# Two weight loads issued by SyncE, a list scheduler that counts SyncE's transfers by their rows, and new order constants, in a fused attention and Mish feed-forward kernel

## The chip, the cores and the metric

The kernel runs on one core of one Trainium2 chip. The metric is the device time of one execution in microseconds (us); the time before is the median of three runs, 942.09 us (940.99 to 942.83). TensorE is called PE, VectorE DVE, ScalarE ACT, GpSimd POOL and SyncE SP, as in the profile.

## The reference

Attention over 8 batches and 8 heads, with 512 local and 32 global positions and a head size of 64. Local queries see a window of 32 to either side and all globals; global queries see everything. A feed-forward layer with w_in (512 x 2048), Mish and w_out (2048 x 512) follows on all 4352 rows.

```python
s_g = scale * np.matmul(q_g, k_all.transpose(0, 1, 3, 2))
out_g = np.matmul(sm(s_g), v_all)
s_ll = np.where(np.abs(pos[:, None] - pos[None, :]) <= 32, scale * np.matmul(q_l, k_l.transpose(0, 1, 3, 2)), -1e9)
a_l = sm(np.concatenate([scale * np.matmul(q_l, k_g.transpose(0, 1, 3, 2)), s_ll], axis=-1))
out_l = np.matmul(a_l, np.concatenate([v_g, v_l], axis=2))
...
h = x @ w_in
sp = np.where(h > 20.0, h, np.log1p(np.exp(np.minimum(h, 20.0))))
return ((h * np.tanh(sp)) @ w_out).astype(np.float32)
```

The weights arrive as 64-bit floats.

## The kernel before, in words

**Attention** runs by units (batch, head pair, quarter of 128 queries), 128 in all: scores `s` on PE (L660), row maximum on DVE (L674), exponential on ACT (L683), split into two float16 halves, transposed (in batch 0 by PE, `PT`, L721, and DVE's L727; later by DMA, `pt`, issued by SP at L548), and multiplied with the values as `U` on PE (L756). DVE normalises U to `x` (L766). In batch 0, x is turned on PE (`XT`) and split into `xh` and `xl` (L743). The values lie in `vraw`; after a maximum over the batch (L560 to L571) they are scaled and split into `vf`, and eight moves per head pair, issued by SP, spread them over `va` and `vc`. U waits for these moves. The global queries have scores `g`, transposes `gpt` and products `gu` (L848).

**Weights** come in 32 loads of 512 KB, 16 for each matrix. Three DVE instructions turn a load's 64-bit floats into 32-bit ones (L466, L473, L475). The first matrix has five load buffers, so load k + 5 waits for the conversion of load k. Each conversion is followed by four small matmuls (`ws`, L487); after the sixteenth a norm goes through DVE (L494), POOL, ACT (a Ln and an Exp, L500 and L501) and DVE to the scale `sw`. Only then is a matrix split into halves: the first one with PE's help (`rest`, L531 and L532), the second one by ACT and DVE (L537). The first five loads are issued by ACT, the others by POOL (`FIRST_ACT`, L450).

**Feed-forward** runs by 17 blocks of 256 rows and 8 steps: `h` (L892, from block 6 on a seven-product form, L1061), Mish on ACT, a split into `G` on DVE or ACT, and `o` (L1125). The first h needs all of `xl` for its rows and the first matrix's halves; the first o needs the second matrix's.

**The order** is made by a list scheduler (`Plan.order`). Each task has an engine, an estimated time, its dependencies and a due number; the scheduler runs a planned clock and always takes the task that can start first, by due number among equals. Its result is the order in which each engine gets its instructions; on the chip each engine runs them in that order and waits where something isn't ready. SP's transfers are the planner's engine DMA: `rows` is the shortest time of an issue there, and its times lengthen where POOL's loads overlap. The due numbers come from constants: `BLK2`, `BLK3`, `LAGX` and `PACE` place the feed-forward steps among the attention units, `CONV1`, `RATE1`, `CONV2` and `RATE2` place the weights' conversions, `FIRST2` and `STEP2` the second matrix's splits.

Of the kernel before, what the change touches and what calls it, by code (L numbers as in the profile page):

```python
# [52 lines left out]
class Plan:  # L53
# [9 lines left out]
    COLD = 2  # L63
    DEEP, ISSUE, SOFT, LANES = 5, 450, 600, 8

# [78 lines left out]
    def order(self):  # L144
# [56 lines left out]
        for _ in range(N):  # L201
# [4 lines left out]
            if self.tasks[n][7] == "dma":  # L206
                s = max(t + self.DMA_IN, late)
                both = min(ns, max(0, moved + self.DMA_IN - s))
                moved += both
                late = s + ns + both  # L210
# [47 lines left out]
def attn_mish_kernel(ctx: ExitStack, tc: tile.TileContext, qt, kt, vm, vg, qg, w1, w2, consts_in, out, w64):  # L258
    nc = tc.nc
# [181 lines left out]
    def w_load(k):  # L441
        j, hf = HV[k]

        def go():
            n = 2 if w64 else 1
            dst = raw(k) if w64 else wf(k).bitcast(I32)
            if k < 16:
                c, f0 = k % 4, k // 4 * 512 * n
                src = w1[c * 128:(c + 1) * 128, f0:f0 + 512 * n]
                (nc.scalar if k < FIRST_ACT else G).dma_start(dst, src if w64 else src.rearrange("p (g f) -> p g f", g=2))  # L450
# [40 lines left out]
    def w_norm(w):  # L491
# [7 lines left out]
        pl.add(DVE, 70, lambda: V.tensor_scalar(X[p], X[p], TINY * TINY, None, ALU.max), w=[p])  # L499
        pl.add(ACT, 94, lambda: A.activation(out=X[p], in_=X[p], func=AF.Ln, bias=0.0, scale=1.0), w=[p], table="exp")  # L500
        pl.add(ACT, 94, lambda: A.activation(out=X[p], in_=X[p], func=AF.Exp, bias=0.0, scale=0.5), w=[p], table="exp")  # L501

# [43 lines left out]
    def turn(kib, dst, src, r, w=(), new=()):  # L546

        pl.add(DMA, kib * 6.8, lambda: nc.sync.dma_start_transpose(dst(), src()), r=r, w=w, new=new, rows=1300)  # L548

    def g_load(b):  # L550
        pl.add(DMA, dma(128), lambda: load(X["qg", b], qg[b]), new=[("qg", ("qg", b))])

    def b_load(b):
        for tag, kib, src in (("vraw", 1024, vm), ("vgraw", 128, vg)):
            pl.add(DMA, dma(kib), lambda tag=tag, src=src: load(X[tag, b], src[b]), new=[(tag, (tag, b))])

# [35 lines left out]
    def k_load(b, hp):  # L592
        pl.add(DMA, dma(320), lambda: load(X["k", b, hp], kt[b, hp]), new=[("k", ("k", b, hp))])

    def q_load(b, hp):
        pl.add(DMA, dma(256), lambda: load(X["q", b, hp], qt[b, hp]), new=[("q", ("q", b, hp))])

# [30 lines left out]
    def v_move(b, hp):  # L628
# [698 lines left out]
    AHEAD_DMA = 12.457  # L1327

# [21 lines left out]
    for i, x in enumerate(ORDER.split()):  # L1350
# [82 lines left out]
```

## Time and profile before

| what | us |
|---|---|
| median of three runs | 942.09 |
| the profiled execution | 942.49 |
| its span, first to last instruction | 940.7 |
| busy: PE / DVE / ACT / POOL | 892.6 / 722.0 / 544.5 / 28.0 |
| mean granted TensorE clock | 0.988 of full speed |

A row of the profile gives start and length, or a count with busy time and the mean of one. A bracket gives the idle time of the engine just before, and what ended it: `[5.36 <-PE U L756]` says that the engine stood still for 5.36 us until PE had written U at line 756. In the table of stretches, PEclk is the granted clock as a part of full speed, and the DMA share is the mean busy share of the core's 16 DMA engines.

### The profile page before, as it was taken

The numbers are of one execution on the slowest core, as the hardware profiler recorded it, in microseconds if no ns is written. First come the engines' busy times: TensorE is split into PE (matmuls) and PEld (weight loads), VectorE is DVE, ScalarE is ACT, GpSimd is POOL, SyncE is SP. The second block draws the span as 40 slices with busy tenths as digits, with TensorE's granted clock in tenths as the row PEclk, the third lists the DMA queues.
The fourth block names the chain that finished last, engine by engine and source line by source line (L and its number), as shares of the span: only waits on it lengthen the run. The fifth ranks groups of instructions, "written<-read, shape, count | busy, mean of one in ns | idle before, by whom it ended". The sixth has DMA issues, their size and how long they took to land.

```text
span 940.7 us, 24081 instructions
## 1 busy us (share of the span) xinstructions
PE 892.6 (95%) x9628; PEld 629.0 (67%) x9628; DVE 722.0 (77%) x1984; ACT 544.5 (58%) x1178; POOL 28.0 (3%) x52
## 2 busy tenths in 40 slices
PE   2668999999999989999999999999999999999997
PEld 1446657767766666767777777777777777767764
DVE  6699886776689998589979977898779766656443
ACT  1446887667787687677666666665666543232111
POOL 5111000000000000000000000000000000000000
PEclk9789999999999999999999999999999999999999
DMA  9966135667874588566556657475565441000000
GB/s 364 301 200 200 51 92 136 129 139 152 189 151 84 129 176 155 121 143 137 107 128 141 145 124 120 117 154 131 106 127 110 83 71 35 1 24 21 4 24 23
DMA packets 214432, 113.96 MB, mean 121 GB/s; under 512 B 181168, under 2 KB 194608, under 8 KB 213296
## 3 DMA queue, kind: packets, MB, share of 16 engines
q1 hardware_dynamic: 209568, 95.39, 46.7%
q0 software_dynamic: 3888, 14.16, 4.3%
q10 hardware_dynamic: 864, 2.88, 0.8%
q8 instruction: 75, 1.23, 0.5%
q14 instruction: 37, 0.30, 0.1%
HBM read 46.32 MB, written 8.91 MB: 59 GB/s over the span
## 4 chain that ended last, share of the span: by engine, by line
PE 81%; DVE 7%; DMA 7%; ACT 3%; SPq 1%; issue 1%; ACTq 0%; DVEq 0%
PE o L1125 36%; PE h L1061 22%; PE h L892 10%; PE s L660 5%; PE U L756 4%; PE g L794 2%; DMA pt<-ph 2%; PE gu L848 2%; DVE W L473 1%; DMA vgraw<-in_vg 1%; DVE W L475 1%; DMA gpt<-gph 1%; DMA W<-in_w 1%; SPq L369 1%; DMA consts<-in_consts 1%
## 5 line engine op out<-in xcount | busy, mean ns | idle before, releaser
L1125 PE MATMUL o<-W,G 128*128 128x512 f16 x1632 | 383.1, 380 | 0.0
L1125 PEld LDWEIGHTS <-G 128*128 128x128 f16 x1632 | 150.3, 98 | 160.3 <-issue 8.4
L683 ACT ACTIVATE P<-P,nm 128x192 f32<-128x192 f32 (+1 forms) x256 | 117.6, 460 | 83.2 <-DVE nm L674 81.6
L1061 PEld LDWEIGHTS <-W 128*128 128x128 f16 x2640 | 153.8, 98 | 16.8 <-issue 0.7
L892 PE MATMUL h<-xh,W 128*128 128x256 f16 x768 | 138.6, 273 | 0.1
L892 PEld LDWEIGHTS <-W 128*128 128x128 f16 x1152 | 109.0, 98 | 20.0 <-issue 3.5
L892 PE MATMUL h<-xl,W 128*128 128x256 f16 x384 | 104.6, 272 | 0.0
L674 DVE CUSTOM_DVE_ANT_0 P<-s,consts 128x192 f32<-128x192 f32 (+1 forms) x256 | 90.0, 367 | 9.5 <-PE PT L721 5.3
L1061 PE MATMUL h<-xh,W 128*128 128x128 f16 x960 | 87.6, 219 | 0.0
L1061 PE MATMUL h<-xl,W 128*128 128x128 f16 x480 | 82.7, 219 | 0.0
L756 PEld LDWEIGHTS <-pt 96*128 96x128 f16 (+1 forms) x1536 | 59.4, 98 | 30.0 <-issue 12.0
L660 PE MATMUL s<-k,q 64*128 64x192 f32 (+1 forms) x512 | 65.5, 372 | 14.5 <-DMA q<-in_qt 12.9
L1085 ACT ACTIVATE VX<-VX,c 128x1024 f32<-128x1024 f32 x22 | 25.3, 1149 | 90.4 <-DVE VX L1082 90.3
L703 DVE SCALAR_TENSOR_TENSOR ph<-P,ph 128x384 f16<-128x384 f32 (+1 forms) x112 | 64.6, 585 | 11.2 <-ACT ph L380 10.6
L1061 PE MATMUL h<-raw,W 128*128 128x128 f16 x1056 | 67.9, 219 | 0.3 <-DVE k L1082 0.3
L756 PE MATMUL U<-va,pt 96*128 96x64 f16 (+1 forms) x720 | 52.9, 193 | 11.8 <-DMA va<-vgf 6.3
L660 PEld LDWEIGHTS s<-k,q 64*128 64x128 f32 x512 | 44.0, 192 | 26.0 <-issue 17.4
L380 ACT ACTIVATE ph<-P 128x384 f16<-128x384 f32 (+1 forms) x108 | 57.0, 540 | 7.2 <-DMA pt<-ph 6.3
L1082 DVE TENSOR_TENSOR k<-h,k 128x512 f32<-128x512 f32 x44 | 30.2, 687 | 38.7 <-PE h L1061 38.5
L756 PE MATMUL U<-vc,pt 96*128 96x64 f16 x768 | 55.6, 193 | 0.0
L1082 DVE TENSOR_TENSOR VX<-h,k 128x512 f32<-128x512 f32 x44 | 30.3, 689 | 30.6 <-PE h L1061 30.1
L683 ACT ACTIVATION_READ_ACCUMULATOR P<-P,nm 128x1 f32 x256 | 47.9, 187 | 0.0
(173 smaller groups left out, 1341.2 us busy)
## 6 DMA issues: line engine op xcount, KB each, us to landing
k<-in_kt SPq DMA_DIRECT2D x32, 320.0 KB, 3.6
W<-in_w POOLq DMA_DIRECT2D x17, 512.0 KB, 7.3
out<-ob SPq DMA_DIRECT2D x33, 256.0 KB, 2.3
q<-in_qt SPq DMA_DIRECT2D x32, 256.0 KB, 3.2
vraw<-in_vm SPq DMA_DIRECT2D x8, 1024.0 KB, 6.0
raw<-in_w POOLq DMA_DIRECT2D x10, 512.0 KB, 4.3
vc<-vf SPq DMA_DIRECT2D x30, 128.0 KB, 2.4
va<-vf SPq DMA_DIRECT2D x30, 96.0 KB, 2.4
```

The costliest lines, as they stand in the source:

```text
L380: A.activation(out=dst, in_=src, func=AF.Copy, scale=c)
L660: T.matmul(X[s[h]][:, cols(u)], X[q][r, u * 128:(u + 1) * 128], X[k][r, c0:c0 + w], start=True, stop=True)
L674: pl.add(DVE, 155 + 1.04 * w, lambda: V.tensor_tensor_reduce(out=half(P, h, w), in0=X[s][:, cols(t)], in1=mask[:, m0:m0 + w], scale=-SCALE ...
L683: pl.add(ACT, 460, lambda: A.activation(out=half(P, h, w), in_=half(P, h, w), func=AF.Exp, bias=X[nm], scale=-1.0, accum_out=X[sums][:, t, ...
L703: pl.add(DVE, dve(n), lambda: V.scalar_tensor_tensor(p_part(X[ph], t, 1), p_src(X[P], t), PSC, p_part(X[ph], t, 0), ALU.mult, ALU.subtract ...
L756: T.matmul(X[u][:, t, h, :], X[pt][:k, p * 4 + h * 2 + c, :], X[vx][:k, t, vl, h * 64:(h + 1) * 64], start=(n == 0), stop=(n == 5))
L794: T.matmul(X[g][half * 64:half * 64 + 64, c0:c0 + n], X[q][:, hp, :], rhs, start=True, stop=True)
L892: T.matmul(X[h][:, f * TB:(f + 1) * TB], wh(i, wl)[:, off:off + 128], X[x][:, d, o:o + TB], start=(n == 0), stop=(n == 11))
L1061: T.matmul(X[h][:, c:c + 128], form(J + jj, wl)[:, off:off + 128], x(l, d), start=(n == 0), stop=(n == 5))
L1082: pl.add(DVE, 720, lambda: V.tensor_tensor(out(), four(P[p])(), x(), ALU.add), r=[P[p]] + list(r), w=list(w), new=new)
L1085: pl.add(ACT, act(1024), lambda: A.activation(out=X[name], in_=X[name], func=AF.Mish, bias=0.0, scale=X[c][:, 0:1]), r=[[c, 0]], w=[name], ...
L1125: T.matmul(X[o], gp(g, blk, i)[:, f, t * 128:(t + 1) * 128], wh(8 + i, wl)[:, f * 512:(f + 1) * 512], start=(turn == 0 and n == 0), stop=( ...
```

## The change

Loads 0 to 2 stay on ACT, loads 3 and 4 go to SP. The planner still books all five on ACT.

```diff
-                (nc.scalar if k < FIRST_ACT else G).dma_start(dst, ...)
+                (nc.scalar if k < 3 else nc.sync if k < FIRST_ACT else G).dma_start(dst, ...)
```

In the planner, a transfer of SP that meets loads of POOL takes twice its time, or 13.5 ns for each of its rows if that is more (`late` is when the planned loads of ACT and POOL end, `moved` when SP's end):

```diff
             if e == DMA:
                 s = max(moved, t)
-                both = min(ns, max(0, late - s - self.DMA_IN))
-                late += both
-                moved = s + ns + both
-                free[e] = max(t + max(self.DMA_MIN, self.tasks[n][6]), moved - self.DMA_AHEAD)
+                busy = late - s - self.DMA_IN
+                slow = max(2 * ns, self.tasks[n][6] % 1000 * self.PER_ROW) if busy > 0 else ns
+                late += min(ns, max(0, busy))
+                moved = s + slow
+                free[e] = max(t + max(self.DMA_MIN, 1300 if self.tasks[n][6] > 1000 else 0), moved - self.DMA_AHEAD)
```

A weight load that overlaps SP's transfers is lengthened by 0.45 of the overlap instead of all of it, and no longer delays them. Loads of q, k, v and the constants get `rows=128`, the moves 32 to 96, the transposes 1128. The norm's Ln and Exp count 200 ns instead of 94. The constants, of which these change most:

```diff
-    BLK2 = 29.169
-    BLK3 = 39.967
-    LAGX = 19.225
+    BLK2 = 27.51
+    BLK3 = 42.58
+    LAGX = 18.0
...
-    PACE = 0.79
+    PACE = 0.9841
...
-    CONV1 = 1.096
-    RATE1 = 0.0
-    CONV2 = 2.335
-    RATE2 = 0.514
+    CONV1 = -0.02276
+    RATE1 = 0.1116
+    CONV2 = 2.074
+    RATE2 = 0.7056
...
-    FIRST2 = 6.491
-    STEP2 = 0.0
+    FIRST2 = 7.245
+    STEP2 = 0.1597
```

No instruction is added or taken away but for a few splits that go from ACT to DVE or back; the order changes on every engine. From line 634 on, the changed kernel's line numbers are higher by one.

Three places show it. The first is the start of SP's program (`in_kt`, `in_qt`, `in_vm`, `in_vg`, `in_w` are k, q, the values, the global values and the weights in memory). Before:

```order
L369 DMA k_98<-in_kt 128x640
L369 DMA q_94<-in_qt 128x512
L369 DMA consts<-in_consts 128x352
L369 DMA vraw_130<-in_vm 128x2048
L369 DMA vgraw_140<-in_vg 128x256
L369 DMA k_99<-in_kt 128x640
L369 DMA q_95<-in_qt 128x512
```

and now:

```order
L369 DMA k_98<-in_kt 128x640
L369 DMA q_94<-in_qt 128x512
L369 DMA consts<-in_consts 128x352
L450 DMA W<-in_w 128x1024 x2
L369 DMA vraw_130<-in_vm 128x2048
L369 DMA vgraw_141<-in_vg 128x256
L369 DMA k_99<-in_kt 128x640
L369 DMA q_95<-in_qt 128x512
```

Both weight loads stand ahead of the first batch's values and of the second head pair's k and q.

The second place is DVE at the first x, in the middle of the first matrix's conversions. Before:

```order
L475 SCALAR_TENSOR_TENSOR W<-W 128x2x256
L466 TENSOR_SCALAR W<-W 128x2x256
L473 SCALAR_TENSOR_TENSOR W<-W 128x2x256
L766 TENSOR_TENSOR x_0_0_397<-U_0_0_361,rs_0_0_211 128x256
L475 SCALAR_TENSOR_TENSOR W<-W 128x2x256
L764 TENSOR_SCALAR rs_2_0_408<-sums_2_0_335 128x4
```

and now (rows with 128x512 convert loads of the second matrix):

```order
L475 SCALAR_TENSOR_TENSOR W<-W 128x2x256
L466 TENSOR_SCALAR W<-W 128x2x256
L473 SCALAR_TENSOR_TENSOR W<-W 128x2x256
L475 SCALAR_TENSOR_TENSOR W<-W 128x2x256
L466 TENSOR_SCALAR W<-W 128x512 x2
L473 SCALAR_TENSOR_TENSOR W<-W 128x512 x2
L466 TENSOR_SCALAR W<-W 128x2x256
L767 TENSOR_TENSOR x_0_0_423<-U_0_0_394,rs_0_0_214 128x256
```

Before, 10 rows of L466, 10 of L473 and 9 of L475 stand ahead of x; now 15, 14 and 12.

The third place is PE at the first o. Before, the last scores of batch 0 stand right ahead of it:

```order
L794 MATMUL g_2_1286<-k_100,qg_207 64x16 x2
L660 MATMUL s_3_1_0_1295<-k_101,q_97 128x224
L660 MATMUL s_3_1_1_1296<-k_101,q_97 128x224
L660 MATMUL s_3_1_0_1295<-k_101,q_97 128x192
L660 MATMUL s_3_1_1_1296<-k_101,q_97 128x192
L1125 LDWEIGHTS G_105
L1125 MATMUL o_0_1310<-W,G_105 128x512
```

and now the seventh step of the first block's h, and a transpose:

```order
L893 MATMUL h_6_1457<-xl_437,W 128x256
L893 LDWEIGHTS W
L893 MATMUL h_6_1457<-xh_433,W 128x256
L722 MATMUL PT_3_2_1497<-consts,P_76 128x128 x4
L1126 LDWEIGHTS G_105
L1126 MATMUL o_0_1514<-W,G_105 128x512
```

Ahead of the first o stand now 24 more matmuls of h, four more halves of `rest` (16 instead of 12), 24 more of U, 18 more of gu, 12 more of PT, and the first scores of batch 1.

More of the change, by code (lines that the diff above doesn't have):

```diff
@@ L63 @@
     COLD = 2
-    DEEP, ISSUE, SOFT, LANES = 5, 450, 600, 8
+    DEEP, ISSUE, SOFT, LANES, PER_ROW = 5, 450, 600, 8, 13.5
     def __init__(self):
@@ L207, in order @@
                 s = max(t + self.DMA_IN, late)
-                both = min(ns, max(0, moved + self.DMA_IN - s))
-                moved += both
+                both = 0.45 * min(ns, max(0, moved + self.DMA_IN - s))
                 late = s + ns + both
@@ L449, in go @@
                 src = w1[c * 128:(c + 1) * 128, f0:f0 + 512 * n]
-                (nc.scalar if k < FIRST_ACT else G).dma_start(dst, src if w64 else src.rearrange("p (g f) -> p g f", g=2))
+                (nc.scalar if k < 3 else nc.sync if k < FIRST_ACT else G).dma_start(dst, src if w64 else src.rearrange("p (g f) -> p g f", g=2))
             else:
@@ L499, in w_norm @@
         pl.add(DVE, 70, lambda: V.tensor_scalar(X[p], X[p], TINY * TINY, None, ALU.max), w=[p])
-        pl.add(ACT, 94, lambda: A.activation(out=X[p], in_=X[p], func=AF.Ln, bias=0.0, scale=1.0), w=[p], table="exp")
-        pl.add(ACT, 94, lambda: A.activation(out=X[p], in_=X[p], func=AF.Exp, bias=0.0, scale=0.5), w=[p], table="exp")
+        pl.add(ACT, 200, lambda: A.activation(out=X[p], in_=X[p], func=AF.Ln, bias=0.0, scale=1.0), w=[p], table="exp")
+        pl.add(ACT, 200, lambda: A.activation(out=X[p], in_=X[p], func=AF.Exp, bias=0.0, scale=0.5), w=[p], table="exp")
         def scale():
@@ L546, in turn @@
     def turn(kib, dst, src, r, w=(), new=()):
-        pl.add(DMA, kib * 6.8, lambda: nc.sync.dma_start_transpose(dst(), src()), r=r, w=w, new=new, rows=1300)
+        pl.add(DMA, kib * 6.8, lambda: nc.sync.dma_start_transpose(dst(), src()), r=r, w=w, new=new, rows=1128)
     def g_load(b):
-        pl.add(DMA, dma(128), lambda: load(X["qg", b], qg[b]), new=[("qg", ("qg", b))])
+        pl.add(DMA, dma(128), lambda: load(X["qg", b], qg[b]), new=[("qg", ("qg", b))], rows=128)
     def b_load(b):
         for tag, kib, src in (("vraw", 1024, vm), ("vgraw", 128, vg)):
-            pl.add(DMA, dma(kib), lambda tag=tag, src=src: load(X[tag, b], src[b]), new=[(tag, (tag, b))])
+            pl.add(DMA, dma(kib), lambda tag=tag, src=src: load(X[tag, b], src[b]), new=[(tag, (tag, b))], rows=128)
     def b_max(b, hp):
@@ L592, in k_load @@
     def k_load(b, hp):
-        pl.add(DMA, dma(320), lambda: load(X["k", b, hp], kt[b, hp]), new=[("k", ("k", b, hp))])
+        pl.add(DMA, dma(320), lambda: load(X["k", b, hp], kt[b, hp]), new=[("k", ("k", b, hp))], rows=128)
     def q_load(b, hp):
-        pl.add(DMA, dma(256), lambda: load(X["q", b, hp], qt[b, hp]), new=[("q", ("q", b, hp))])
+        pl.add(DMA, dma(256), lambda: load(X["q", b, hp], qt[b, hp]), new=[("q", ("q", b, hp))], rows=128)
     def loc(k, j, n):
@@ L632, in mv @@
         def mv(kib, dst, src, r, w, new=()):
-            pl.add(DMA, dma(kib), lambda: load(dst(), src()), r=[r], w=[w], new=new)
+            rows = {32: 64, 128: 64, 48: 32, 96: 64, 16: 32}[kib] + (64 if r == g and kib == 48 else 0)
+            pl.add(DMA, dma(kib), lambda: load(dst(), src()), r=[r], w=[w], new=new, rows=rows)
         mv(32, lambda: X[va][0:64, 0], lambda: X[vf][0:64, 0], vf, [va, 0], [("va", va)])
@@ L1165, in attn_mish_kernel @@
     LATER = 24
-    BOOST = 84.202
+    BOOST = 84.2
     BOOST2 = -11.635
@@ L1318, in attn_mish_kernel @@
     LOADS1 = 0.038
-    CONV1 = 1.096
-    RATE1 = 0.0
-    CONV2 = 2.335
-    RATE2 = 0.514
+    CONV1 = -0.02276
+    RATE1 = 0.1116
+    CONV2 = 2.074
+    RATE2 = 0.7056
     FIRST1 = 6.564
     STEP1 = 1.0
-    FIRST2 = 6.491
-    STEP2 = 0.0
-    AHEAD_DMA = 12.457
+    FIRST2 = 7.245
+    STEP2 = 0.1597
+    AHEAD_DMA = 12.46
     def weights():
@@ L1359, in attn_mish_kernel @@
         elif a == "m":
-            pl.add(DMA, 500, lambda: load(consts, consts_in), w=["consts"])
+            pl.add(DMA, 500, lambda: load(consts, consts_in), w=["consts"], rows=128)
         elif a == "g":
```

## The prediction

> **What bounds the kernel now.** I read the page first, then a table of stretches, then the waits in the first 120 us one by one. The page gives the span, the share of each engine and PE's course in 40 slices of 23.5 us:
>
> ```profile
> span 940.7 us, 24081 instructions
> PE 892.6 (95%) x9628; PEld 629.0 (67%) x9628; DVE 722.0 (77%) x1984; ACT 544.5 (58%) x1178; POOL 28.0 (3%) x52
> PE   2668999999999989999999999999999999999997
> ```
>
> PE is the bound, and it runs the same matmuls before and after the change: no line of the diff adds or removes one. So the time can only move where PE waits or has a low clock. The table of stretches says where that is (columns: stretch, its length, busy us and count of PE, PEld, DVE, ACT and POOL, granted PE clock, DMA share, GB/s):
>
> ```profile
> 0.00:40.00 40.00, 15.57 (x82) 9.60 (x83) 26.42 (x75) 13.15 (x36) 15.74 (x30) 0.93 0.98 361
> 40.00:60.00 20.00, 12.71 (x120) 8.73 (x120) 16.16 (x39) 4.57 (x11) 1.72 (x3) 0.76 0.75 209
> 60.00:80.00 20.00, 17.42 (x135) 10.15 (x134) 19.70 (x64) 13.15 (x32) 3.04 (x6) 0.95 0.52 177
> 80.00:120.00 40.00, 36.85 (x326) 26.26 (x324) 34.77 (x109) 29.60 (x57) 3.68 (x7) 0.96 0.39 113
> 120.00:200.00 80.00, 80.00 (x722) 54.13 (x721) 60.99 (x186) 60.15 (x130) 0.35 (x1) 1.00 0.54 120
> 200.00:260.00 60.00, 57.91 (x586) 40.28 (x585) 40.43 (x145) 42.67 (x101) 0.00 (x0) 1.00 0.73 163
> 320.00:360.00 40.00, 36.75 (x376) 26.26 (x375) 37.54 (x121) 31.40 (x73) 0.72 (x1) 1.00 0.85 173
> 440.00:930.00 490.00, 489.83 (x5925) 355.28 (x5925) 366.29 (x912) 244.49 (x516) 2.15 (x3) 1.00 0.42 88
> ```
>
> PE idles 24.4 us before 40 us, 7.3 in the next 20, 2.6 and 3.2 in the two rows after; later only 2.1 and 3.3 in two pockets. After 440 us there is nothing to gain. In the first 40 us the DMA engines are full (0.98), and from 60 us DVE is (19.70 of 20). Between the two lies one hole where both PE and DVE stand still:
>
> ```profile
> 36.37 0.69 DVE L473 SCALAR_TENSOR_TENSOR W<-W 128x512 int32<-128x512 int32 x1
> 42.42 0.42 DVE L766 TENSOR_TENSOR x<-U,rs 128x256 f32<-128x256 f32 x1 [5.36 <-PE U L756]
> 40.95 0.32 PE L756 MATMUL U<-va,pt 96*128 96x64 f16 x3 [6.27 <-DMA va<-vgf]
> 48.45 0.53 POOL L450 DMA_DIRECT2D W<-in_w  x1 [4.06 <-DVE W L466]
> ```
>
> DVE works in program order, and the first x (L766) stands ahead of weight conversions that need nothing from PE. So 5.36 us pass until PE has U, which waits for the moves of the first values. The last load of the first matrix, issued by POOL only once DVE has freed its buffer, goes out at 48.45.
>
> **The change part by part.** *The order on DVE at the first x* is the largest term. Ahead of it the new order has five more L466, four more L473 and three more L475, and the same other rows:
>
> ```profile
> L475 DVE SCALAR_TENSOR_TENSOR W<-W 128x512 int32<-128x512 int32 x19 | 13.0, 684 | 0.1
> L473 DVE SCALAR_TENSOR_TENSOR W<-W 128x512 int32<-128x512 int32 x18 | 12.3, 684 | 0.1
> L466 DVE TENSOR_SCALAR W<-W 128x512 int32<-128x512 int32 x17 | 7.0, 419 | 0.0
> ```
>
> 5 x 0.419 + 7 x 0.684 = 6.9 us of work stands where 5.36 us of waiting stood. DVE ended its last conversion at 37.06, so it reaches x at 37.06 + 6.9 = 44.0. Is U there by then? SP now issues the second pair's large move (vc<-vf, 128 KB) ahead of the rest of the first pair's moves (here one move, then the three that end the first pair's). The trace does not show that order; the nearest rows are these:
>
> ```profile
> 31.11 0.59 SPq L369 DMA_DIRECT2D vc<-vf  x1
> 32.51 4.35 SPq L369 DMA_DIRECT2D va<-vgf  x3
> ```
>
> One more move costs SP between 0.6 us (the row at 31.11) and 4.35 / 3 = 1.5 us (the row at 32.51); I take 1.5, since the queues are full there. x could then start at 42.42 + 1.5 = 43.9, and DVE meets it without a wait. The 6.9 us done early are missing later, so DVE is ahead by 42.42 + 6.9 - 44.0 = 5.3 us. What is late next are the last weights of the first matrix: their loads go out earlier because their buffers are freed earlier, but into full queues. For them I take off 1.3 us (bounds 0 and 5.3) and keep **-4.0 us** for everything that DVE sets from there on. Up to the xl that the first h (L892) waits for, DVE's rows are the same to within 0.5 us in both orders, so the first h moves from 79.1 to 75.1 us.
>
> *The first o (L1125).* These rows show the end of the start-up (of L892, the starts of its first and last matmul):
>
> ```profile
> 112.08 0.15 DVE L386 TENSOR_SCALAR wp<-wp 128x1 int32<-128x1 int32 x1 [3.19 <-ACT wp L501]
> 114.42 1.28 DVE L537 SCALAR_TENSOR_TENSOR W<-W,sw 128x1024 f16<-128x1024 f32 x1 [0.44 <-ACT W L380]
> 114.98 0.97 PE L660 MATMUL s<-k,q 64*128 64x224 f32 x6 [1.61 <-ACT xg L380]
> L892 PE MATMUL h<-xh,W x768: 270/273/283, 79.1 to 425.4; 128*128 128x256 f16 x192
> 115.88 8.34 PE L1125 MATMUL o<-W,G 128*128 128x512 f16 x30
> 115.00:120.00 5.00, 5.00 (x18) 2.19 (x19) 4.77 (x15) 4.04 (x7) 0.00 (x0) 0.66 0.54 150
> ```
>
> PE waits 1.61 us for a PSUM buffer, and the clock drops right behind it: 0.66 over 5 us is 5 x 0.34 = 1.7 us lost. In the new order those scores stand far earlier, and before the first o PE does more: 24 matmuls of h, four more halves of rest, one more group of s, and others. Their price, from the chain of work (start, length, what):
>
> ```profile
> 157.14 3.93 PE h L892 x36
> 89.41 1.01 PE rest L531 x2
> 90.42 0.22 PE rest L532
> ```
>
> 24 x 3.93 / 36 = 2.6, 4 x 1.23 = 4.9, and some 4.3 for s, 24 small U, 18 gu, a g and three PT: 11.8 us, an estimate. PE goes from the first h to the first o in 115.9 - 79.1 = 36.8 us now; then in 36.8 - 1.6 + 11.8 = 47.0, so the first o starts at 75.1 + 47.0 = 122.1. From there the old run took 940.7 - 115.9 = 824.8 us; less 11.8 done already and 1.7 of low clock, 811.3. That is a span of **933.4**. The 11.8 goes in and out again, so the span doesn't hang on it: it is 940.7 less 4.0, 1.6 and 1.7.
>
> What hides the first o's weights: the first L537 stands behind 41 more DVE rows, about 12 us by their durations, but 4.0 us are gained ahead and 3.6 us of waits (3.19 + 0.44) get filled, which makes 114.4 + 12 - 7.6 = 118.8, ahead of PE's 122.1. That cover is only 3 us thick, so I add an allowance of **+2.0** (bounds 0 and 7.5, the first rival below).
>
> *The fourth and fifth load on SP.* They now stand ahead of vraw, k and q of the second pair:
>
> ```profile
> q10 hardware_dynamic: 543, 2.02, 43.2%
> q1 hardware_dynamic: 656, 1.90, 42.4%
> 2.12 0.84 SPq L369 DMA_DIRECT2D vraw<-in_vm  x1
> vraw<-in_vm SPq DMA_DIRECT2D x1, 1024.0 KB, 9.9
> DMA packets 2115, 5.62 MB, mean 402 GB/s; under 512 B 234, under 2 KB 534, under 8 KB 2114
> q1 hardware_dynamic: 1055, 1.75, 33.6%
> 16.61 0.43 DVE L466 TENSOR_SCALAR W<-W 128x512 int32<-128x512 int32 x1 [2.95 <-DMA W<-in_w]
> ```
>
> Until 12 us SP's queue (q1) and ACT's (q10) share evenly. vraw, issued at 2.1 and 9.9 under way, lands at 12.0. With 1.05 MB put ahead of it, it lands 2.6 us later if q1 gets what q10 leaves (1.05 MB at 402 GB/s), or 8.4 us later at q1's own rate between 16 and 30 us (1.75 MB in 14 us): at 14.6 or 20.4. Its first reader waits now for the fifth weight (L466 at 16.61) and starts at about 17. So the cost lies between a gain of 2.95 us (that wait) and a loss of 3.4; I take 0, nearer to the first rate, since q10 is empty by then.
>
> The Trainium skill, DMA: Bandwidth & Descriptors, section "Issuing engines are not separate DMA queues", says that loads from different engines run on the same 16 DMA engines and only save issue time; by it this part alone is worth nothing, and the sum stays as it is. The trace agrees in so far as both queues together reach what one had later (402 GB/s).
>
> *The pockets.* PE's waits between 200 and 440 us:
>
> ```profile
> PE U L756 <- DMA pt<-ph: 3.7, 4, 2.0
> PE gu L848 <- DMA gpt<-gph: 1.1, 2, 0.8
> ```
>
> Counted with the durations of their rows, the new order leaves DVE 6 to 15 us less to do ahead of the transposes of the 320 to 360 pocket, and PE at most 9 less ahead of the U that read them; around 230 us PE has 4 to 8 us more to do before each U. So these 4.8 us shrink rather than grow; I take **-1.0** (bounds -4.8 and +3, the 320 to 360 pocket once more).
>
> The two ACT rows (200 instead of 94 ns), the turn's rows and the other row counts change only the planner's times. Sum: 933.4 + 2.0 - 1.0 = 934.4 us of span; the profiled execution took 942.5, 1.8 more than its span, and lay 0.4 above the median of 942.1. So 934.4 + 1.8 - 0.4 = 935.8, said as **936**.
>
> **The rivals.** *The second norm takes over (no change).* In the new order ACT's second Ln (L500) stands behind two more Mish, two more weight halves, and some small ones:
>
> ```profile
> L938 ACT ACTIVATE EE<-h,c 128x512 f32<-128x512 f32 x6 | 4.1, 686 | 2.2 <-PE h L892 2.1
> L380 ACT ACTIVATE W<-W,sw 128x1024 f16<-128x1024 f32 x13 | 14.9, 1144 | 0.7 <-DVE W L537 0.6
> ```
>
> That is 2 x 0.69 + 2 x 1.14, and about 8.3 us for casts, a table load, vf parts and scalings: 12 us, an estimate. For: ACT is busy 29.60 of 40 us there. Against: it has 10 idle us, and its inputs come 4 us earlier. If nothing is hidden, the first o comes 12 us later than now, at 127.9: PE waits 5.8 us and pays the low clock (1.7) again: 933.4 + 7.5 + 1.8 - 0.4 = **942.3**.
>
> *SP's queue starves the values (slower).* If q1 keeps its own rate, vraw, sv, vf and the moves come 8.4 us later and one move more (1.5): the first U goes from 40.95 to 50.9, x to 52.3, and DVE stands still from 44.0. DVE is then 52.3 - (42.42 + 6.9) = 3.0 us behind the old run instead of 4.0 ahead, a swing of 7.0: 933.4 + 7.0 + 2.0 + 1.4 = **943.8**, and up to 949 with the second norm's wait on top. It is slower than before once vraw lands after about 20 us, or the first U starts after 49. For: q1 had a third of the engines from 16 us. Against: two queues shared evenly before, and q10 ends early. The same page of the Trainium skill, section "Queues, rings and completion order", has each DMA engine take turns between the queues that have work. By it this rival holds only while POOL's queue is fed; the trace shows that from 16 us.
>
> *The pockets close as well (faster still).* All 4.8 us go and the allowance isn't used: 933.4 - 4.8 + 1.4 = **930.0**. For: the orders there. Against: a chain of transposes behind a 1 MB load stays in SP's order.
>
> *The change doesn't do what it says:* the planner still books both loads on ACT while SP issues them. The order of SP shows them there, so this falls.
>
> **How the numbers follow.** Forecast, 934 to 939.5: 0.58. Second norm, 939.5 to 943: 0.18. Queue starved, 943 to 949: 0.14. Pockets closed, below 934: 0.10. The range 930.5 to 943 leaves out the starved queue and little of the last. A measurement can tell about 0.2% (1.9 us) from no change: faster than 940.2 takes the forecast, the closed pockets and a little of the second norm, 0.72; within 0.2%, 0.16; slower than 944.0, most of the starved queue, 0.12.
>
> **What would show it.** Right: no wait at DVE's first x, or one under 1.5 us; the first h near 75 us; the first o near 122 us with no PE wait ahead of it and a clock of 1.00 there; vraw's reader at 17 us. Wrong: the first U after 45 us (queue), PE idle over 3 us before the first o (norm), or waits of PE for pt above 6 us between 200 and 440 us.

## The result, and the profile after

The changed kernel takes **948.4 us** (median of 10 runs, 946.2 to 952.3) where the kernel before takes 943.4 (10 runs, 940.7 to 946.9). The ratio is 1.0054, with a 95% interval of 1.0034 to 1.0074: **slower by half a per cent**, where 936 us had been forecast. The profiled execution took 947.2 us, 4.7 more than that of the kernel before. PE is still the bound, with the same matmuls, and waits more:

```profile
span 945.4 us, 24030 instructions
PE 892.9 (94%) x9628; PEld 627.3 (66%) x9628; DVE 721.5 (76%) x1979; ACT 547.0 (58%) x1182; POOL 26.7 (3%) x52
PE   3588899999999999999899999999999999999997
```

The table of stretches of the changed kernel (columns as in the prediction: stretch, length, busy us and count of PE, PEld, DVE, ACT and POOL, granted PE clock, DMA share, GB/s):

```profile
0.00:40.00 40.00, 19.23 (x98) 11.77 (x99) 31.14 (x84) 13.66 (x36) 16.18 (x32) 0.92 0.99 361
40.00:60.00 20.00, 11.70 (x120) 8.08 (x119) 14.45 (x42) 5.38 (x17) 1.98 (x3) 0.74 0.54 159
60.00:80.00 20.00, 16.11 (x150) 9.91 (x150) 19.81 (x64) 15.12 (x37) 2.74 (x5) 1.00 0.81 235
80.00:120.00 40.00, 36.57 (x352) 26.82 (x350) 35.20 (x110) 26.38 (x48) 3.54 (x7) 1.00 0.45 136
120.00:200.00 80.00, 76.53 (x658) 50.04 (x657) 56.83 (x176) 57.87 (x131) 0.35 (x1) 1.00 0.52 107
320.00:360.00 40.00, 39.51 (x360) 26.67 (x357) 37.72 (x104) 27.87 (x61) 0.52 (x1) 1.00 0.66 146
440.00:460.00 20.00, 16.40 (x247) 13.08 (x245) 17.83 (x47) 13.79 (x29) 0.00 (x0) 0.92 0.89 161
```

PE does 3.7 us more in the first 40 us and loses less at 320 to 360 us (0.5 for 3.25). But it idles 3.5 us between 120 and 200 us, where it was full before, and 3.6 us between 440 and 460 us, with a low clock behind. The same 20 us of the kernel before were nearly full:

```profile
440.00:460.00 20.00, 19.83 (x292) 16.17 (x292) 19.13 (x56) 13.34 (x30) 0.72 (x1) 1.00 0.67 136
```

**A measure for orders that differ.** PE's time up to some instruction can't be compared where other work stands ahead of it. So I take the *lost time* at a mark: its start less the work that PE did before it, with each matmul counted at its own issue interval at full clock (from the rows of the kernel before: an o 0.217 us, an h 0.111, one of the seven-product h 0.057, a U 0.031, an s 0.113 and so on). Its level depends on these prices; what counts are the differences between kernels. "U 69" is the first U of the 69th of 128 attention units, near 426 us, "U 77" that of the 77th, near 480. Kernels whose names begin with b_ are the one before with an edit, those with a_ the changed one with an edit; they come up below.

| kernel | first U | first h | h of the second block (155 us) | U 69 | U 77 | end | ratio to before (95%) |
|---|---|---|---|---|---|---|---|
| before | 31.8 | 48.3 | 55.1 | 62.4 | 62.9 | 62.2 | 1 |
| **changed** | 35.5 | 45.3 | 54.5 | 61.6 | 67.5 | 66.8 | 1.0054 (1.0034 to 1.0074) |
| a_act | 33.9 | 43.7 | 55.3 | 63.2 | 67.1 | 66.8 | 1.0057 (1.0039 to 1.0075) |
| b_sync | 34.4 | 51.8 | 57.6 | 66.8 | 67.5 | 66.7 | 1.0028 (1.0011 to 1.0045) |
| a_oldconst | 34.5 | 46.5 | 58.1 | 66.7 | 67.2 | 66.5 | 1.0028 (1.0016 to 1.0041) |
| a_vraw5 | 35.0 | 46.6 | 54.2 | 62.3 | 66.2 | 65.5 | 1.0032 (1.0012 to 1.0052) |
| a_lag19 | 36.4 | 47.7 | 56.9 | 78.0 | 78.4 | 77.7 | 1.0138 (1.0115 to 1.0160) |
| a_oldff | 36.0 | 45.9 | 58.9 | 70.7 | 71.4 | 70.6 | 1.0047 (1.0031 to 1.0064) |
| a_oldw2 | 36.4 | 50.6 | 67.2 | 73.4 | 79.9 | 79.8 | 1.0159 (1.0138 to 1.0180) |
| a_more | 35.6 | 46.7 | 57.3 | 62.4 | 66.7 | 66.0 | 1.0039 (1.0024 to 1.0054) |
| a_u69 | 35.6 | 47.1 | 54.9 | 60.2 | 70.5 | 69.9 | 1.0115 (1.0093 to 1.0138) |
| b_x | 30.6 | 46.8 | 53.6 | 62.2 | 62.7 | 62.0 | 0.9978 (0.9965 to 0.9991) |
| b_x2 | 30.6 | 47.6 | 53.3 | 62.2 | 62.7 | 62.0 | 0.9984 (0.9972 to 0.9995) |
| b_v4 | 31.9 | 48.6 | 54.0 | 59.9 | 60.8 | 60.1 | 0.9984 (0.9973 to 0.9996) |
| b_x2v4 | 32.8 | 48.4 | 54.2 | 61.7 | 62.3 | 61.6 | 0.9979 (0.9968 to 0.9990) |

A row is one profiled execution, the ratio comes from many. How far one row can be trusted is in the table itself: the changed kernel, a_lag19, a_vraw5, a_more and a_u69 have one and the same order up to the second block, and scatter by 1.4 us at the first U, 2.4 at the first h and 3.1 at the second block's h. Five such rows average 46.7 and 55.6 there; the two of the old order (before, b_v4) average 48.5 and 54.6. So the start-up gains **1.8 us** up to the first h, and by 155 us **nothing is left of it** (the difference of 1.0 the other way lies within the scatter). The changed kernel's own row gains 3.0 at the first h; the four others have a slot of half the clock between 72 and 77 us, right ahead of the first h, which costs 1.7 us, and it has none. From 155 us to U 69 the new order gains about 1 us, less than the scatter, and behind it the changed kernel loses 5.2 where the old order loses nothing.

**The start.** DVE's wait at the first x is as long as before, though 4.7 us more work of DVE lie in the first 40 us:

```profile
14.80 0.69 DVE L560 TENSOR_REDUCE vmx<-vraw 128x1 f32<-128x512 f32 x1 [0.40 <-DMA vraw<-in_vm]
47.14 0.42 DVE L767 TENSOR_TENSOR x<-U,rs 128x256 f32<-128x256 f32 x1 [5.48 <-PE U L757]
```

The values are read at 14.8 us, earlier than before, and yet the first U comes at 45.7.

**Between the first h and the first matmuls of o** PE waits at five places for about a microsecond each (start, length, what, and in brackets the wait before it):

```profile
88.23 0.20 PE L757 MATMUL U<-va,pt 128*128 128x64 f16 x1 [0.81 <-DVE pt L728]
96.96 0.41 PE L487 MATMUL ws<-W 128*128 128x128 bf16 x4 [0.76 <-DVE W L475]
98.95 1.13 PE L531 MATMUL rest<-W,dg 128*128 128x512 f32 x2 [1.37 <-ACT EE L939]
126.28 0.63 PE L722 MATMUL PT<-consts,P 128*128 128x128 f32 x4 [0.84 <-DVE rs L766]
128.04 1.24 PE L1126 MATMUL o<-W,G 128*128 128x512 f16 x5 [0.92 <-DVE W L537]
```

The wait of 1.61 us for s and the low clock of 1.7 us at 116.6, which the kernel before has here, are gone as forecast. These five make 4.7 us; with two smaller ones PE waits 5.9 us from the first h to this o, 2.9 in the kernel before.

**The hole at 446 to 460 us.** DVE waits for the values of batch 5, PE behind DVE, and then a U for its transposes:

```profile
444.38 0.69 DVE L560 TENSOR_REDUCE vmx<-vraw 128x1 f32<-128x512 f32 x1 [1.62 <-DMA vraw<-in_vm]
446.93 0.22 PE L1062 MATMUL h<-xh,W 128*128 128x128 f16 x1 [1.17 <-DVE VX L1083]
453.23 0.25 PE L757 MATMUL U<-vc,pt 96*128 96x64 f16 x3
455.91 0.26 PE L757 MATMUL U<-va,pt 128*128 128x64 f16 x3 [2.43 <-DMA pt<-ph]
456.28 5.74 PE L1126 MATMUL o<-W,G 128*128 128x512 f16 x18
```

PE ran two U of one head pair right behind each other and 18 matmuls of o after them. In the order in which PE ran them (batch 4, third head pair, then block 6; matmuls in brackets) the kernel before has work between those U:

```
before:   U (12)  s (8)  h_6 (24)  o_6 (12)  h_6 (24)  o_6 (6)  U (12)  o_6 (6)  h_6 (24)  U (12)
changed:  h_6 (24) x5  U (12)  g (8)  s (8)  U (12)  U (12)  o_6 (18)  h_6 (24)  o_6 (6)
```

The h of block 6 are done before the U, and the U wait in a row.

### The profile page after: what moved, and what is told of

Its sections match the earlier page's. It is cut to its first block, busy times and chain, and to the rows that moved or that the text cites. A ratio compares the mean times of both kernels' runs of the same rounds, so it can differ in the third digit from the quotient of the medians.

```text
span 945.4 us, 24030 instructions
## 1 busy us (share of the span) xinstructions
PE 892.9 (94%) x9628; PEld 627.3 (66%) x9628; DVE 721.5 (76%) x1979; ACT 547.0 (58%) x1182; POOL 26.7 (3%) x52
## 3 DMA queue, kind: packets, MB, share of 16 engines
q1 hardware_dynamic: 209856, 96.44, 47.7%
## 4 chain that ended last, share of the span: by engine, by line
PE 71%; DVE 12%; DMA 11%; ACT 4%; issue 1%; SPq 1%; DVEq 0%; ACTq 0%
PE o L1126 31%; PE h L1062 21%; PE h L893 7%; PE s L661 4%; PE U L757 4%; DMA pt<-ph 3%; DMA va<-vf 2%; PE g L795 1%; PE gu L849 1%; DVE P L675 1%; DMA q<-in_qt 1%; DMA vraw<-in_vm 1%; DMA va<-vgf 1%; DVE W L473 1%; DVE W L475 1%
## 5 line engine op out<-in xcount | busy, mean ns | idle before, releaser
L757 PEld LDWEIGHTS <-pt 96*128 96x128 f16 (+1 forms) x1536 | 58.9, 98 | 32.2 <-issue 16.7
L661 PEld LDWEIGHTS s<-k,q 64*128 64x128 f32 x512 | 43.9, 192 | 21.1 <-issue 12.9
```

Of the source, the lines that this page charges most:

```text
L661: T.matmul(X[s[h]][:, cols(u)], X[q][r, u * 128:(u + 1) * 128], X[k][r, c0:c0 + w], start=True, stop=True)
L757: T.matmul(X[u][:, t, h, :], X[pt][:k, p * 4 + h * 2 + c, :], X[vx][:k, t, vl, h * 64:(h + 1) * 64], start=(n == 0), stop=(n == 5))
```

## The experiments

### Who issues the two loads: a_act and b_sync

a_act is the changed kernel with

```diff
-                (nc.scalar if k < 3 else nc.sync if k < FIRST_ACT else G).dma_start(dst, ...)
+                (nc.scalar if k < FIRST_ACT else G).dma_start(dst, ...)
```

> The changed kernel with loads 3 and 4 issued by ACT again, the order of every engine otherwise the same. Theory C (the two loads on SP delay the first values, so that the first U comes at 45.7 us): vraw's reader starts 2 us earlier or more, the first U at 42 to 43.5 us, and what DVE sets from there comes 2 to 3 us earlier: 945.4 to 946.5 us. Rival D (the moves of the first values are late because POOL's queue is fed earlier and fuller, whoever issues loads 3 and 4): the first U stays at 45 to 46 us and the time within 1 us of the changed kernel's 948.4.

b_sync is the kernel before with the opposite edit.

> The kernel before with loads 3 and 4 issued by SP, nothing else. Theory C: vraw lands 2 to 8 us later, the first U moves from 40.95 to 43 to 47 us and the time rises by 1 to 3 us: 944.5 to 946.5. Rival D: DVE waits for the fifth weight no longer and for the values as long; the first U within 1 us of 40.95 and the time within 1 us of 943.4.

The first U of a_act and of b_sync, and in b_sync the first reader of vraw:

```profile
44.04 0.32 PE L757 MATMUL U<-va,pt 96*128 96x64 f16 x3 [3.27 <-DMA va<-vgf]
```

```profile
43.58 0.32 PE L756 MATMUL U<-va,pt 96*128 96x64 f16 x3 [9.80 <-DMA va<-vgf]
14.76 0.69 DVE L560 TENSOR_REDUCE vmx<-vraw 128x1 f32<-128x512 f32 x1 [1.21 <-DMA vraw<-in_vm]
```

In the kernel before, the two loads on SP alone delay the first U by 2.6 us (40.95 to 43.58) and cost 0.28% (946.4 us beside 943.5 in the same runs). Theory C holds there for the first U and for the time, though not by its mechanism, since vraw is read *earlier* with the loads on SP (14.76 for 16.95). It is the moves behind them that come late. Of the three that SP issues at 32.51 us in the kernel before (shown in the prediction), b_sync has this row:

```profile
35.18 3.79 SPq L369 DMA_DIRECT2D va<-vgf  x3
```

That is 2.7 us later, although DVE has written vgf 0.9 us earlier (at 23.7 us for 24.6). What holds SP up in between was not settled.

In the changed order taking the loads off SP brings the first U 1.6 us forward, to 44.0, between C's range and D's; the time stays what it was, 948.3, as D had it. DVE keeps these 1.6 us until 89 us and then loses them, and 0.7 more, at a load of the second matrix:

```profile
91.73 0.43 DVE L466 TENSOR_SCALAR W<-raw 128x512 int32<-128x512 int32 x1 [2.64 <-DMA raw<-in_w]
```

In the changed kernel the same row waits 0.29 us. What the start had gained stopped at this load.

### The rules without the constants: a_oldconst

The changed kernel with all constants of the order set back.

> The changed kernel with all constants as before: only the planner's rules and the two loads on SP are left of the change. Theory L (the rules by themselves move little): as the kernel before with the two loads on SP, 945.5 to 947.5 us, with the first U at 43 to 45 us. Rival M (the rules let the planner see SP's late moves, and it fills the gap): the first U at 43 to 45 us, but the first h at 79 us or earlier and 942 to 944 us.

945.7 us, a ratio as that of b_sync: theory L for the time. The new rules do move the start, as rival M had it: the first h comes at 77.5 us, 82.7 in b_sync. But at 155 us that is gone (58.1 and 57.6 in the table), and with the old constants the rules neither help nor cost anything that can be measured in the time. What the changed kernel loses beyond that (1.0054 beside 1.0028, with intervals that just overlap) goes with the new constants. It does not need the two loads on SP: a_act, which has the constants without them, is as slow.

### The hole: a_lag19, a_vraw5, a_oldff

```diff
-    LAGX = 18.0
+    LAGX = 19.225
```

> The changed kernel with the old LAGX (19.225 for 18.0), so that the feed-forward from block 4 on is due one attention unit later again; the order up to about 300 us stays that of the changed kernel. Theory A (the loss is made where the seven-product blocks begin, by the feed-forward being due one unit earlier there): PE's waits of 1.2 and 2.4 us at 446 to 456 us and the low clock behind them (1.7 us) go, 4.2 us less than the changed kernel: about 944.2 us. Rival B (the loss is spread over the start-up and the blocks before 440 us, the hole only shows it): the waits turn up elsewhere, 947 to 949 us.

Neither time: 957.4 us. After 440 us PE loses nothing any more, but between 335 and 358 us it loses 16:

```profile
345.31 0.26 PE L757 MATMUL U<-va,pt 96*128 96x64 f16 x3 [2.17 <-DMA pt<-ph]
351.63 0.34 PE L757 MATMUL U<-va,pt 128*128 128x64 f16 x3 [4.62 <-DMA pt<-ph]
355.03 0.37 PE L893 MATMUL h<-xh,W 128*128 128x256 f16 x1 [2.58 <-ACT EE L939]
```

This date moves every step from block 4 on. The hole is gone, and a larger one stands where the old dates meet the new order.

a_vraw5 moves two tasks in the finished order:

```diff
-        for n in self.order():
+        seq = self.order()
+        ...   # L619 of batch 4's last values 16 DVE tasks earlier, vraw of batch 5 8 rows of SP earlier
+        for n in seq:
```

> The changed kernel with two instructions moved and nothing else: the low half of batch 4's last values (L619) 16 tasks earlier on DVE, and the load of batch 5's values that waits for it (vraw) 8 rows earlier on SP, from 437 to about 428 us. If the late load is what makes the hole at 446 to 456 us, DVE's wait of 1.6 us for vraw goes and with it PE's 1.2 and 2.4 us and the 1.7 us of low clock: 943.2 to 944.5 us. If the block sums that DVE does there (L1021, L1025) are the cause and the load only one of their victims, PE's wait of 2.4 us for pt stays and at most 1.6 us go: 946.8 to 948 us.

DVE's wait for vraw is gone. PE still waits, 0.87 us for gpt, and for the same U:

```profile
456.33 0.26 PE L757 MATMUL U<-va,pt 128*128 128x64 f16 x3 [2.27 <-DMA pt<-ph]
```

946.5 us, 1.9 less than the changed kernel, with intervals that overlap. The second reading held (the time is just under its range): the late load was not what makes the larger wait. (The low clock behind it did not come this time; more on that at the end.)

a_oldff has the old BLK2, BLK3, LAGX and PACE.

> The changed kernel with the four feed-forward constants (BLK2, BLK3, LAGX, PACE) as before; the order is the changed kernel's up to about 75 us. Theory J (these constants make the hole at 446 to 460 us and with the start-up of the changed kernel the old ones do as well as before): no such hole, PE's lost time after 440 us within 0.5 us, 942 to 944.5 us. Rival K (each set of constants fits only the clock it was found with, as the run with LAGX alone shows): holes elsewhere after 200 us, 950 us or more.

947.2 us: the hole is gone (0.7 us between U 69 and U 77), but by 155 us the kernel has lost 4.4 us more than the changed one, 4.7 more go between there and U 69, and a pocket near 352 us is back:

```profile
354.48 0.26 PE L757 MATMUL U<-va,pt 128*128 128x64 f16 x3 [2.61 <-DMA pt<-ph]
```

J is right that the hole goes and wrong about the sum; K is right that time is lost elsewhere, and its 950 us is too much. (The profiled execution was the slowest of seven, 3.8 us above the median.)

### The hole by its own dates: a_more and a_u69

Only the steps of the seven-product blocks move here. MORE says by how many units they are put back; in a_more they have the date they had before the change:

```diff
-    MORE = 3.68
+    MORE = 4.68
```

> The changed kernel with MORE = 4.68 for 3.68: only the steps of the seven-product blocks (from block 6 on) are due one attention unit later, which is the date they had before; the order stays that of the changed kernel up to about 415 us. Theory Q (in the changed kernel the h of block 6 are due one unit too early, so that PE has done them when the units of batch 4 are still waiting for their transposes, and nothing is left to put between these units): the o of block 6 stand between the units' U again, PE waits under 1 us between 440 and 460 us, and the time falls by 3 to 5 us, to 943.5 to 945.5. Rival R (DVE is full from 405 to 456 us and sets the pace in any order): PE's lost time between 425 and 485 us stays at 4 us or more, 947 to 949.

a_u69 sends the first steps of block 6 the other way:

```diff
-        pl.late = BOOST if u < 70 else BOOST2
+        pl.late = BOOST if u < 69 else BOOST2
```

> The changed kernel with the limit below which the feed-forward is put back (u < 70) set to 69, so that the first steps of block 6, which are due at 69, lose that and run further ahead; the order stays that of the changed kernel up to about 410 us. Theory Q: more h of block 6 are done early, three U of one head pair stand in a row, and PE's wait ahead of them grows: 2 us or more lost beyond the changed kernel, 950 to 953. Rival R: as the changed kernel, 947 to 949.5.

PE's waits of a_u69, and then those of a_more, in the same place:

```profile
455.23 0.26 PE L757 MATMUL U<-va,pt 128*128 128x64 f16 x3 [3.52 <-DMA pt<-ph]
459.20 0.34 PE L757 MATMUL U<-va,pt 128*128 128x64 f16 x3 [3.44 <-DMA pt<-ph]
```

```profile
443.14 0.26 PE L757 MATMUL U<-va,pt 128*128 128x64 f16 x3 [1.51 <-DMA pt<-ph]
444.47 0.34 PE L849 MATMUL gu<-gpt,va 128*128 128x64 f16 x3 [0.80 <-DMA gpt<-gph]
```

With the steps further ahead, PE's two waits for pt make 7.0 us and the time grows to 952.3 us, as theory Q said; its interval lies clear of the changed kernel's. With the old date PE's waits there fall from 3.6 to 2.3 us and the time is 946.4, outside both ranges; the intervals of a_more and the changed kernel overlap, so that a gain in time is not shown. So the dates of block 6 have a share in the hole, shown in one direction, and most of it remains when they alone go back.

The table says where the rest may lie. Between U 69 and U 77 the three runs with the old LAGX (a_lag19, a_oldff, a_oldconst) lose 0.4 to 0.7 us, as the kernel before, and the six with the new one 3.9 to 10.3. LAGX also moves blocks 4 and 5, which a_more leaves at their new dates; no run moves these two alone. R's reason is not enough: DVE is as full in the kernel before (47.7 of 51 us from 405 to 456 us, 48.5 in the changed one), and PE hardly waits there.

### The second matrix's dates: a_oldw2

```diff
-    CONV2 = 2.074
-    RATE2 = 0.7056
+    CONV2 = 2.335
+    RATE2 = 0.514
...
-    FIRST2 = 7.245
-    STEP2 = 0.1597
+    FIRST2 = 6.491
+    STEP2 = 0.0
```

> The changed kernel with the second matrix's four constants (CONV2, RATE2, FIRST2, STEP2) as before: its conversions and splits are spread over fewer attention units. From about 165 us on the order on every engine is the changed kernel's again, so the hole at 446 to 460 us stays as it is. Theory H (the spread conversions of the second matrix cost what was gained, 3.8 us between the first h and 170 us): the waits of PE between 94 and 131 us shrink by 3 to 4 us and the time falls to 944.5 to 945.5 us. Rival I (DVE and ACT are full there in any order): other waits take their place, 947.5 to 949.5.

957.8 us, against both. The first o now stands earlier than its weights:

```profile
112.93 0.58 PE L1126 MATMUL o<-W,G 128*128 128x512 f16 x1 [3.97 <-ACT W L380]
114.64 1.86 PE L1126 MATMUL o<-W,G 128*128 128x512 f16 x4 [1.12 <-DVE W L537]
```

PE loses 16.6 us between the first h and the second block's h (67.2 less 50.6), where the changed kernel loses 9.2. So the new dates of the second matrix do not cost what was gained; in the changed order they keep the first o behind its weights.

### The first x alone: b_x and b_x2

b_x takes the prediction's largest term by itself, in the kernel before: nine conversions moved ahead of the first x.

> The kernel before with nine weight conversions on DVE (those of loads 9 to 11, and the first ones of two loads of the second matrix that lie there since about 20 us; 5.1 us of work by the trace's durations) moved ahead of the first x, and nothing else. Theory E (the wait at the first x is free time for DVE, as the prediction had it): the first U stays within 1.5 us of 40.95, the first h comes 3.5 to 4.5 us earlier (75 us), and the time falls to 939 to 941 us. Rival F (the wait is one for the DMA engines, which are full until 45 us: conversions done earlier free their buffers, POOL issues two more weight loads, 1 MB or 2.9 us at 363 GB/s, ahead of the moves of the first values): the first U moves to 43 to 44.5 us, the first h comes only 1 to 2.5 us earlier, and the time is 941 to 942.5. Rival G (the gain is given back before 170 us, where DVE and ACT are full): the first h earlier as in E or F, but the time within 1 us of 943.5.

The first U came at 39.8 us and the first h at 77.7, against E and F. In this run the conversion of the first load of the second matrix writes over load 11 before that is converted, so a part of the first matrix gets other values; the number and kind of the instructions stay the same. b_x2 keeps these in order.

> As b_x, but with the conversions moved in the order in which they stood (all of loads 9 to 11, then the first row of each of two loads of the second matrix, 5.0 us), so that load 11 is converted before its place is written again. Theory N (what stood in the gap at the first x also filled the gaps behind it, between x, XT, PT and pt; taking it away leaves these open, so that only 1.5 of 5 us stay): the first U below 41.5 us, DVE idle 3 us or more between 42 and 50 us, the first h at 77 to 78.3 us. Then, as PE's course in b_x shows, 1.5 to 2.5 us of lead until 320 us, of which the pocket at 330 to 354 us takes most back: 941 to 942.8 us. Rival E (all of the 5 us stay): the first h at 75 to 76 us and 939 to 940.5 us.

The first x of b_x2 has no wait. But DVE then stands still four times, where before the edit it had these conversions to do:

```profile
42.73 0.42 DVE L766 TENSOR_TENSOR x<-U,rs 128x256 f32<-128x256 f32 x1
44.33 0.42 DVE L743 TENSOR_TENSOR xl<-XT,xh 128x256 f16<-128x256 f32 x1 [0.69 <-ACT xh L373]
46.91 0.36 DVE L674 CUSTOM_DVE_ANT_0 P<-s,consts 128x192 f32<-128x192 f32 x1 [2.16 <-PE PT L721]
47.97 0.69 DVE L727 SCALAR_TENSOR_TENSOR pt<-PT,pt 128x512 f16<-128x512 f32 x1 [0.69 <-ACT pt L380]
49.48 0.69 DVE L727 SCALAR_TENSOR_TENSOR pt<-PT,pt 96x512 f16<-96x512 f32 x1 [0.82 <-ACT pt L380]
```

That is 4.4 us. The kernel before stands still twice in the same rows, for 1.4 us:

```profile
44.03 0.42 DVE L743 TENSOR_TENSOR xl<-XT,xh 128x256 f16<-128x256 f32 x1 [0.29 <-ACT xh L373]
45.87 0.36 DVE L674 CUSTOM_DVE_ANT_0 P<-s,consts 128x192 f32<-128x192 f32 x1 [1.09 <-PE PT L721]
```

Both kernels then come to the same conversion, the tenth behind the first x of the kernel before (its row first, then that of b_x2):

```profile
51.38 0.68 DVE L473 SCALAR_TENSOR_TENSOR W<-W 128x512 int32<-128x512 int32 x1
50.70 0.68 DVE L473 SCALAR_TENSOR_TENSOR W<-W 128x512 int32<-128x512 int32 x1
```

Of the 5.0 us DVE is 0.7 ahead, and it stays so up to the first h, which comes at 78.4 us, 0.7 earlier than before. In b_x it comes 1.4 us earlier, and in b_x2v4 (below), which has the edit of b_x2, 0.2 later. The time falls by 0.22% in b_x and 0.16% in b_x2. Theory N holds but for its first h, late by 0.1 us: the wait at the first x was real, but the work that could fill it was already filling the gaps behind it. (In b_x2 a part of the gap of 2.16 us may be PE's clock, which was at half until 49.1 us, in the kernel before until 44.9. In b_x it rose at 45.5, and DVE still stood 4.1 us in these gaps.)

### The pocket at 345 us: b_v4 and b_x2v4

Two tasks moved in the kernel before, as in a_vraw5, here the low half of L619 that frees vraw 8 tasks earlier on DVE and vraw of batch 4 four rows earlier on SP.

> The kernel before with two instructions moved: the low half (L619) that frees vraw 8 tasks earlier on DVE, and the load of batch 4's values (vraw, 1 MB) four rows earlier on SP, from 338 to about 335 us, so that it is mostly through before the two transposes behind it (5.15 us of issue at 339.4 us). Theory O (the pocket at 345 to 347 us is made by transposes that stand in SP's queue behind this load): the transposes are issued in 3 to 4 us, PE's wait of 2.0 us there falls below 0.8 us, DVE's wait for vraw (1.2 us) goes, and the time falls by 1 to 2 us: 941.3 to 942.5. Rival P (the DMA engines are full from 335 to 347 us whatever the order): the waits move to gpt or to the next pt, 943 to 944.

SP's rows around that load, before and then in b_v4 (start and time of issue):

```profile
338.15 0.58 SPq L369 DMA_DIRECT2D vraw<-in_vm  x1
339.36 5.15 SPq L548 DMA_TRANSPOSE pt<-ph  x2
```

```profile
333.76 0.53 SPq L369 DMA_DIRECT2D vraw<-in_vm  x1
338.27 3.58 SPq L548 DMA_TRANSPOSE pt<-ph  x2
344.47 0.26 PE L756 MATMUL U<-va,pt 128*128 128x64 f16 x3 [0.52 <-DMA pt<-ph]
```

The issue of the two transposes takes 3.6 us for 5.15 and PE waits 0.52 us for 2.0, and DVE's wait for vraw is gone: theory O. The time is 940.9 us, 0.16% less.

> Both edits of b_x2 and b_v4 in the kernel before. Theory O: the lead of the start-up passes the pocket at 330 to 354 us, and the two gains add: 939 to 941 us. Rival P: PE's lost time at 354 us is that of the kernel before (62.3 us) again, 941.5 to 943 us.

941.3 us, a ratio of 0.9979: faster than both kernels of this case, but no more than either edit reaches alone within the intervals. That the two gains add was not shown.

## Why the prediction was wrong

By the lost times of the two profiles, the forecast and the measured change part like this (us; minus is faster):

| stretch | forecast | measured |
|---|---|---|
| up to the first h | -4.0 | -3.0 |
| first h to the second block's h | -1.6 - 1.7 + 2.0 = -1.3 | +2.4 |
| from there to U 69 | -1.0 | -0.2 |
| U 69 to the end | 0 | +5.4 |
| sum | -6.3 | +4.6 |

**The wait at DVE's first x (-4.0 us): the steps that failed are "x could then start at 42.42 + 1.5 = 43.9, and DVE meets it without a wait" and "keep -4.0 us for everything that DVE sets from there on".** The x started at 47.14 and DVE waited 5.48 us for it, as long as before. By the prediction's own formula that leaves 42.42 + 6.9 - 47.1 = 2.2 us of lead, not 5.3. Half of the 3.2 us by which x was late are the two loads, which the sum had at 0: with them on ACT (a_act) x starts at 45.5. The other half comes on top of the 1.5 us that were priced for SP's order of moves, and was not taken apart. That the first h came at 75.9 all the same, near the 75.1 forecast, is in part luck: the four other profiles of this order have it at 77.2 to 78.3. It came early by another way than the one given: DVE had 4.7 us more work done at 40 us, and had no more gaps right behind x, where it had stood still 1.4 us before. What the step is worth by itself b_x, b_x2 and b_x2v4 show, in the old order: of 5 us of work moved into the wait, nothing to 1.4 us remained, because that work had filled the gaps behind. And the lead did not last: a_act lost 1.6 us of it at one weight load, and over five profiles nothing is left at 155 us.

**The two loads on SP (0): they cost 1.6 us at the first U, by another way than the one that was priced.** vraw, issued at 5.08 us, landed at 14.8, at the early end of its bounds (14.6), and was read at once, not at 17. The moves that follow on the same queue were late all the same. Nor is the 402 GB/s of the prediction's row what one queue had: from 16 to 30 us POOL's queue moved 3.86 MB and SP's 1.75. The Trainium skill, DMA: Bandwidth & Descriptors, section "Issuing engines are not separate DMA queues", has the choice of the issuing engine save only issue time. b_sync differs from it: moving the two loads, and with them the order in SP's queue, cost 0.28% here, and the measurement decides.

**The first o (-3.3 us, allowance +2.0): the wait and the low clock that were named did go, but the allowance was for the wrong cover.** It was meant for the second norm: the weights were to be ready at 118.8 us and PE at 122.1. Both were late, by 8 and 5 us:

```profile
107.18 0.14 DVE L499 TENSOR_SCALAR wp<-wp 128x1 f32<-128x1 f32 x1
121.82 0.20 ACT L500 ACTIVATE wp<-wp 128x1 f32<-128x1 f32 x1
126.70 1.28 DVE L537 SCALAR_TENSOR_TENSOR W<-W,sw 128x1024 f16<-128x1024 f32 x1 [0.48 <-ACT W L380]
```

Fourteen us lie between the norm's step on DVE and its Ln on ACT, which stands behind the work that the prediction had listed for it. PE came late enough itself to wait only 0.92 us for these weights. What it had been late for are mostly the 3 us of small waits at 87 to 99 us, which no step of the prediction looked for: it had counted what PE does ahead of the first o, and not whether DVE and ACT, busy 35.2 and 26.4 of 40 us there, deliver each piece in time. a_oldw2 shows what the norm rival's mechanism does where it isn't avoided: 5.1 us of waiting at the first o.

**The pockets from 200 to 440 us (-1.0): the waits shrank as forecast.** PE's idle time in gaps of over 0.25 us, summed over 200 to 440 us, fell from 5.2 to 3.5 us (2.9 to 5.0 in four other profiles with the changed order up to there), and the pocket at 345 us went. In lost time less is left of it, since PE lost 1.6 us between 155 and 170 us. The reason given, less work on DVE ahead of the transposes, was not tested. b_v4 shows that in the kernel before the pocket came from transposes that wait behind a 1 MB load in SP's order. The prediction expected this chain to stay; the changed order has parted it by almost 8 us:

```profile
341.80 0.58 SPq L369 DMA_DIRECT2D vraw<-in_vm  x1
349.54 2.67 SPq L548 DMA_TRANSPOSE pt<-ph  x2
```

**After 440 us: the step that failed is "After 440 us there is nothing to gain".** True, and it was read as if there were nothing to lose. The new dates change the order to the end, and no place after 440 us was compared. There 5.4 us were lost against the kernel before, more than the whole result (in a_act and a_vraw5, which have the same order on PE, 3.8 and 3.4). That the new feed-forward dates make the hole is shown by a_u69 in one direction. The three runs with the old LAGX, which don't have it, agree, but are no clean comparison, since each of them had lost 5 to 16 us more than the changed kernel by U 69. How much of the hole belongs to which block stays open.

Of the rivals, the starved queue had the right sign and, at 943.8 to 949, the right range, and its sign, a first U after 45 us, came true (45.7). But that was luck: no value was late, and a_act, with the first U at 44.0, is as slow. The second norm gave 942.3 and cost 0.9 us; its sign, PE idle over 3 us before the first o, came true by other waits.

## What to carry to other kernels

A wait that gets filled is worth only what is left over once the gaps that the moved work filled before are open again: read the next ten rows of that engine, not only the row with the wait. A lead at the start counts only as far as the next thing that does not move with it, here a load of weights. In a scheduled program, a constant that helps one stage has a place in every later one; compare the order also where the profile of before is full, since a stretch without waits is one that can only get worse. And constants found together hold only together: of the four partial returns to the old ones (a_lag19, a_oldff, a_oldw2, a_more) two were far worse than the change and two could not be told from it.

## What was not expected of the hardware

**The clock falls by a grid, not by a wait.** In all 15 traces the granted clock is either full or half, and changes on a grid of 3.41 us. I took, for each slot of that grid after 60 us that ran at full clock, the time without a matmul, and whether the next slot was at half clock:

| idle in a slot of 3.41 us | slots | next slot at half clock |
|---|---|---|
| under 1.5 us | 3756 | 0 |
| 1.5 to 2.0 us | 29 | 13 |
| 2.0 us and more | 15 | 15 |

Of the 3756, PE was without a pause in all but 282. At half clock one o follows the other every 427 ns, at full clock every 216, so a full slot at half clock costs 1.7 us. A wait of 2.4 us then costs 2.4 us if it falls evenly across two slots, and 4.1 if it lies in one. The changed kernel's wait at 453.5 us was of the second kind, that of a_vraw5 of the first; this alone is most of the difference between their traces after 440 us (5.2 and 3.2 us). It also goes far to explain b_x2, whose 2.26 us at 345 us were followed by such a slot where the 2.0 us of the kernel before were not, and which so lost in the trace what it wins in the timed runs. The Trainium skill, TensorE: Matmul & The Clock Gate, section "What's actually happening", has this free-running window of 3413 ns, and the traces agree; it has the clock fall after one idle window, where here 2.0 us of idle in a window were always enough.

**One order, many times.** Runs of one kernel lie 6 us apart (946.2 to 952.3, 940.7 to 946.9), in a_vraw5 10 (943.4 to 953.8). That is as much as several such slots; no run shows that these are what makes it. A difference below 2 us between two single traces says little without a second pair.
